# Moving work between engines in the start of a fused attention and expert kernel

## The chip, the cores and the metric

One NeuronCore of a Trainium2 chip runs the whole program; the other cores are idle. The metric is the device time of one execution in microseconds (us), as the median of several runs. Below, PE is TensorE (matmuls), ACT is ScalarE, DVE is VectorE, POOL is GpSimd, and SP is SyncE, which only issues DMAs.

## The reference

Three stages follow each other. The first is a linear attention with a delta rule: for every head a state matrix is read by the query and then corrected by the key, step by step over 768 positions. The second is a gated product of three matmuls, the third a mixture of 8 experts, where each token goes to one expert.

```python
for t in range(S):
    kt, vt, bt = (k_n[:, :, t], v[:, :, t], beta[:, :, t, None])
    y[:, :, t] = np.einsum('bhd,bhde->bhe', q[:, :, t], state)
    v_old = np.einsum('bhde,bhd->bhe', state, kt)
    state = state + bt[:, :, :, None] * np.einsum('bhd,bhe->bhde', kt, vt - v_old)
...
h = a * b @ w3              # a = x @ w1, b = x @ w2
return (h @ w_out)
...
e_idx = np.argmax(logits, axis=1)   # logits = x @ w_gate + modality_bias
out[mask] = gate_w[mask, None] * (np.maximum(x[mask] @ w1[e], 0.0) @ w2[e])
```

B = 4 batches, H = 8 heads, S = 768 positions, D = 48 per head; 3072 tokens of 384, inner width 1024.

## The kernel before, in words

**Attention in chunks.** The 768 positions are cut into 12 steps of 64, and two steps make a unit (6 units). Within a unit the recurrence becomes a triangular system for each of 64 pairs of heads and chunks. `gram` forms the products of keys on PE and copies them, negated, into `An`. `inverse` inverts the 32x32 diagonal blocks on DVE: it transposes the blocks (`Ab`), takes the norms of the keys from the diagonal (`ss`, a square root on ACT, then a chain of small operations for `r`), scales by beta (`bt`), and then runs 31 pairs of operations (`tmp`, then `T`), a product and a sum each, both with two SBUF inputs. At the end T is multiplied by beta and transposed back into `An` and, a second time, into `TT`. `merge1` and `merge2` make 64x64 blocks out of the 32x32 ones with matmuls (`pe`, `pf`) and copies of their results. `inverse` is a generator: each `yield` ends a step, and the callers say how many steps are taken where.

**One attention step s** is a chain: `chain_k` (keys times state, subtracted from the values that `scaled` multiplied by the key norms; result R), `chain_u` (TT times R into X), `chain_y` (the output, with the masked query products W, into yT and from there by DMAs into x), and `chain_s` (the new state). `masked` multiplies keys by queries on PE (`pq`) and writes the strictly causal part to W, by a DVE product with a 0/1 mask.

**The fused loop.** `moe1(i)` treats 256 tokens in 8 blocks f: 18 matmuls `pAB`, a product on DVE, and 6 matmuls `px` that run two blocks behind. Ahead of each block `slot(i + 1, f)` puts one piece of attention step i + 1. PLAN and PLAN1 say how many steps of the next unit's inverse go into each block (PLAN1 for the first token group). Then follow the experts (`moe2`), which the change does not touch.

**The startup** (line 522 on) must have the weights and attention step 0 ready before `moe1(0)`. It goes through a list of 36 loads: 8 pieces of w_out, 16 of w3, 12 of w1 and w2. Tick n takes one: `scalar(n + 1)` (two ACT passes that turn the 64-bit words of the next piece into fp32 parts), `vector(n)` (two DVE operations that merge them), `flush(n)` (copies that are now due) and `use(n)` (matmuls). `do[n]` adds the attention pieces to tick n: steps of the first inverse in ticks 1, 4, 6 and, by START0, 8 to 16; merge1, merge2 and the chain of step 0 from tick 17 on, one per tick (CHAIN); the second unit's key products at FC + 9 + GRAMS, that is in ticks 19 to 22; steps of the second inverse (WORK1) in the last four ticks; the routing constants in ticks 9 to 11. `split` puts a matmul piece into one tick and its copies into the next. REST says how many ticks are left to the first blocks of `moe1(0)`: two before.

**The order of the work** is set by hand: `Engine` (line 74) chains every instruction of an engine to the one before it, so each engine, SP and POOL too, runs its instructions in exactly the order in which the program issues them. POOL has little in its queue and so runs ahead of the others. PSUM tiles of one tag alternate between two buffers.

Of the kernel before, what the change touches and what calls it, by code (L numbers as in the profile page):

```python
# [15 lines left out]
AF = mybir.ActivationFunctionType  # L16
# [37 lines left out]
MID = (0,) * 5 + (0, 0, 1) + (2, 2, 2, 1, 1, 1, 1, 2)  # L54
PLAN1 = (3, 4, 4, 4, 5, 4, 4, 2)
WORK1 = (1, 1, 1, 1)
AHEAD, W0 = 8, 0
CHAIN, GRAMS = (1, 1, 1, 1, 1, 1), (2, 3, 4, 5)
START0 = (4, 4, 4, 4, 4, 4, 4, 4, 2)

REST = (1, 1)
EARLY = (4, 2)
# [41 lines left out]
class Kernel:  # L104
# [182 lines left out]
    def gram(self, u, a):  # L287

        nc, a1, ps = self.nc, self.a1, self.ps
        st = self.st[u]
        if "An" not in st:
            st["An"] = a1.tile([P, NU, C], F32, tag=f"An{(u + 1) % 2 if u else 0}", name="An")
        An, kT = st["An"], st["kT"]
        pg = ps.tile([P, HP, C], F32, tag="ps", name="pg")
        for n in range(HP):
            for h in range(2):
                o, w = (1 - h) * C, h * C  # L300
                nc.tensor.matmul(pg[o:o + C, n], kT[w:w + C, a + n], kT[w:w + C, a + n], start=True, stop=True)
        yield
        nc.scalar.activation(An[:, a:a + HP], pg, AF.Copy, scale=-1.0)

        for h in range(2):
            o = h * C + 32
            nc.scalar.activation(An[o:o + 32, a:a + HP, 0:32], pg[o:o + 32, :, 32:64], AF.Copy, scale=-1.0)
# [9 lines left out]
    def scaled(self, s):  # L317
        u, c = divmod(s, US)
        vt = self.st["v", s]
        self.nc.gpsimd.tensor_tensor(out=vt, in0=vt, in1=self.st[u]["r"][:, c * NP:(c + 1) * NP].unsqueeze(2).to_broadcast([P, NP, D]), op=ALU.mult)  # L320

    def inverse(self, u):
# [6 lines left out]
        nc.gpsimd.memset(T, 0.0)  # L329
        nc.gpsimd.memset(T.rearrange("p a b -> p (a b)")[:, 0:1024:33], 1.0)  # L330
        nc.vector.transpose(Ab.rearrange("n j i -> n i j"), An[:, :, 0:32].rearrange("j n i -> j i n"))

        ss, r, r2, rb = (a2.tile([P, 32], F32, tag=x, name=x) for x in ("ss", "r", "r2", "rb"))
        nc.vector.tensor_scalar(out=ss, in0=Ab.rearrange("p a b -> p (a b)")[:, 0:1024:33], scalar1=-1.0, scalar2=0.0, op0=ALU.mult, op1=ALU.max)
        nc.scalar.activation(r, ss, AF.Sqrt)
        yield
# [10 lines left out]
        st["r"] = rb  # L347
        nc.vector.tensor_tensor(out=Ab, in0=Ab, in1=bt.unsqueeze(2).to_broadcast([P, 32, 32]), op=ALU.mult)
        yield
        tmp = a1.tile([P, 256], F32, tag="tmp", name="tmp")  # L350
        for j in range(31):
# [5 lines left out]
            yield  # L357
        nc.vector.tensor_tensor(out=T, in0=T, in1=bt.unsqueeze(1).to_broadcast([P, 32, 32]), op=ALU.mult)

        nc.vector.transpose(An[:, :, 0:32].rearrange("i n c -> i c n"), T)  # L360
# [9 lines left out]
    def merge1(self, u):  # L370

        nc, A, todo = self.nc, self.st[u]["An"], []
        for c in range(0, NU, NP):
            pe = self.ps.tile([P, NP, 32], F32, tag="ps", name="pe")
            for n in range(NP):
                for h in range(2):
                    a, bb = h * C, h * C + 32
                    nc.tensor.matmul(pe[bb:bb + 32, n], A[a:a + 32, c + n, 32:64], A[a:a + 32, c + n, 0:32], start=True, stop=True)
            todo.append((c, pe))
        yield  # L380
        for c, pe in todo:
            for h in range(2):
                bb = h * C + 32
                nc.scalar.copy(A[bb:bb + 32, c:c + NP, 0:32], pe[bb:bb + 32])

    def merge2(self, u):
# [9 lines left out]
        for c, pf in todo:  # L396
            for h in range(2):
                a = h * C
                nc.scalar.copy(TT[a:a + 32, c:c + NP, 32:64], pf[a:a + 32])

# [8 lines left out]
    def masked(self, s):  # L409
# [13 lines left out]
        for a, pq in todo:  # L423
            for h in range(2):
                o = (1 - h) * C
                nc.vector.tensor_tensor(out=W[o:o + C, h, a:a + HP], in0=pq[o:o + C], in1=mb[o:o + C], op=ALU.mult)

# [23 lines left out]
    def chain_u(self, s):  # L451
# [10 lines left out]
        for a, pu in todo:  # L462
            for h in range(2):
                o = (1 - h) * C
                nc.scalar.copy(X[o:o + C, h, a * D:(a + HP) * D], pu[o:o + C])

    def chain_s(self, s):
# [10 lines left out]
        for a, pS in todo:  # L478
            for h in range(2):
                w = h * C  # L480
                if s == 0:
                    nc.scalar.copy(X2[w:w + D, h, a * D:(a + HP) * D], pS[w:w + D])
                    continue
# [3 lines left out]
    def chain_y(self, s):  # L487
# [15 lines left out]
        for a, py in todo:  # L503
            nc.scalar.copy(yT[:, a:a + HP], py)
            p0, p1 = a // B, (a + HP) // B
# [16 lines left out]
    def startup(self):  # L522
# [153 lines left out]
        for x in range(0, NU, HP):  # L676
            do.setdefault(FC + len(START0) + GRAMS[x // HP], []).append(lambda x=x: split(self.gram(1, x)))
        do.setdefault(t, []).append(lambda: setattr(self, "work", self.inverse(1)))
        for n, k in enumerate(WORK1, NSTART - len(WORK1)):
            do.setdefault(n, []).extend([lambda: next(self.work)] * k)  # L680
        rs = self.routing_setup()
        for x in range(3):
            do.setdefault(FC + 1 + x, []).append(lambda: next(rs, None))
        do.setdefault(t + 3, []).append(lambda: self.parts_x(0))
# [653 lines left out]
```

## Time and profile before

| | |
|---|---|
| Median of 3 runs | 857.78 us (857.75 to 859.2) |
| The profiled execution | 855.77 us, span 854.0 us |
| Busy over the span | PE 796.9, DVE 613.7, ACT 409.6, POOL 162.7 us |
| Mean granted clock of PE | 0.966 |

The span runs from the first to the last instruction of the profiled execution; its own time is 1.8 us longer. A wait is put down to what came last before the waiting instruction started. Times of matmuls are modelled, so a busy PE is not PE at its peak. The startup takes the first 129 us; the fused loop runs to about 610 us, the experts to the end.

### The profile page before, as it was taken

To read this page: it belongs to the slowest core of one execution; us is meant where nothing else is said; L and a number is where in the kernel's file an instruction comes from. 1 tells how busy PE (TensorE), PEld (TensorE's weight loads), DVE (VectorE), ACT (ScalarE), POOL (GpSimd) and SP (SyncE) were. 2 spreads that over 40 slices of the span, in tenths; PEclk is the share of its full clock that TensorE was granted. 3 is DMA by queue.
4 is the path that set the end of the run, shared out by engine and by line. 5 is a ranking of instruction groups with operands and counts; after the bars stand their busy time and mean duration, and the time that the engine had idled before them with its cause. 6 is when DMAs were issued, how large, how long until landed. Compare 5 with 4: busy or idle time off the path is not lost.

```text
span 854.0 us, 24817 instructions
## 1 busy us (share of the span) xinstructions
PE 796.9 (93%) x10223; PEld 739.6 (87%) x10223; DVE 613.7 (72%) x1512; ACT 409.6 (48%) x863; POOL 162.7 (19%) x174
## 2 busy tenths in 40 slices
PE   3977879989999999999999999999899999999994
PEld 3844638988999999999999999999899999999983
DVE  3897399969866986698669874457786678667651
ACT  6525964462445344624462444335555565655541
POOL 5000300010001000100010000003244564545420
PEclk8588979999999999999999999999999999999998
DMA  9835434303220322032202121028457768667620
GB/s 301 289 102 186 126 98 135 83 17 85 71 82 6 98 71 83 21 87 80 68 26 78 39 64 40 2 90 264 128 157 247 243 229 267 227 211 249 223 63 6
DMA packets 48777, 105.42 MB, mean 123 GB/s; under 512 B 9412, under 2 KB 28756, under 8 KB 48656
## 3 DMA queue, kind: packets, MB, share of 16 engines
q1 hardware_dynamic: 41424, 88.35, 33.5%
q0 software_dynamic: 4064, 11.06, 3.8%
q10 hardware_dynamic: 3168, 4.34, 1.4%
q8 instruction: 82, 1.34, 0.7%
q14 instruction: 39, 0.32, 0.1%
HBM read 89.15 MB, written 10.63 MB: 117 GB/s over the span
## 4 chain that ended last, share of the span: by engine, by line
PE 62%; DVE 8%; issue 8%; POOL 4%; ACT 1%; DMA 1%; SPq 0%; POOLq 0%; ACTq 0%; DVEq 0%
PE pAB L84 23%; PE px L84 14%; PE ph L84 7%; PE spy L84 4%; PE py L84 2%; PE pq L84 2%; PE pk L84 2%; PE pu L84 2%; PE pS L84 2%; POOL w1l L84 2%; PE pg L84 1%; PE pe L84 1%; DVE Tt L84 1%; POOL out_dram L84 1%; DVE tmp L84 1%
## 5 line engine op out<-in xcount | busy, mean ns | idle before, releaser
L84 PE MATMUL pAB<-x,w 128*128 128x256 f32 x1728 | 231.3, 288 | 0.0
L84 PEld LDWEIGHTS pAB<-x,w 128*128 128x128 f32 x1728 | 214.6, 192 | 4.1
L84 ACT CAST ch<-a 128x256 fp32r<-128x256 f32 x96 | 38.9, 406 | 117.7 <-DVE a L84 117.7
L84 ACT COPY a<-pAB 128x256 f32<-128x256 f32 x96 | 35.7, 372 | 124.5 <-PE pAB L84 118.4
L84 DVE TENSOR_TENSOR a<-a,pAB 128x256 f32<-128x256 f32 x96 | 39.9, 416 | 73.6 <-ACT a L84 73.4
L84 PE MATMUL ph<-sxh,w1h 128*128 128x256 f32 x288 | 82.1, 285 | 0.5 <-DVE hl L84 0.5
L84 PE MATMUL ph<-sxh,w1l 128*128 128x256 f32 x288 | 80.8, 281 | 0.0
L84 PE MATMUL ph<-sxl,w1h 128*128 128x256 f32 x288 | 80.8, 280 | 0.0
L84 ACT ACTIVATE hh<-ph 128x256 fp32r<-128x256 f32 x96 | 37.0, 385 | 89.1 <-PE ph L84 88.7
L84 DVE TENSOR_TENSOR Tt<-tmp,Tt 128x31 f32<-128x31 f32 (+15 forms) x186 | 63.8, 343 | 6.6 <-DVE tmp L84 0.2
L84 DVE SCALAR_TENSOR_TENSOR hl<-ph,hh 128x256 fp32r<-128x256 f32 x96 | 40.2, 419 | 39.0 <-ACT hh L84 37.7
L84 DVE TENSOR_TENSOR w2l<-r,w2h 128x768 fp32r<-128x768 f32 x56 | 59.3, 1071 | 12.3 <-ACT w2h L84 12.1
L84 DVE TENSOR_TENSOR tmp<-Ab,Tt 128x31 f32<-128x31 f32 (+15 forms) x186 | 65.4, 352 | 3.2
L84 PE MATMUL px<-w34h,ch 128*128 128x392 f32 x192 | 65.8, 343 | 0.8 <-DVE w34l L84 0.8
L84 PE MATMUL px<-w34h,cl 128*128 128x392 f32 x192 | 65.3, 340 | 0.0
L84 PE MATMUL px<-w34l,ch 128*128 128x392 f32 x192 | 65.2, 339 | 0.0
L84 POOL TENSOR_TENSOR w1l<-r,w1h 128x512 fp32r<-128x512 f32 x39 | 50.5, 1313 | 50.4 <-ACT w1h L84 50.2
L84 POOL TENSOR_TENSOR vt<-vt,rb 128x768 f32<-128x768 f32 x12 | 18.2, 1519 | 201.6 <-DMA vt<-in_v_dram 117.7
L84 PEld LDWEIGHTS ph<-sxh,w1h 128*128 128x128 f32 x288 | 54.3, 188 | 1.3 <-DVE hl L84 1.1
L84 PE MATMUL pw<-wosW,TT 128*128 128x392 f32 x80 | 37.0, 605 | 19.5 <-DVE TT L84 19.2
L84 DVE TENSOR_TENSOR cl<-a,ch 128x256 fp32r<-128x256 f32 x96 | 40.4, 421 | 19.6 <-ACT ch L84 18.8
L84 PEld LDWEIGHTS ph<-sxh,w1l 128*128 128x128 f32 x288 | 54.3, 189 | 0.0
(262 smaller groups left out, 1742.9 us busy)
## 6 DMA issues: line engine op xcount, KB each, us to landing
r<-in_e_w_dram SPq DMA_DIRECT2D x42, 512.0 KB, 4.7
r<-in_e_w_dram SPq DMA_DIRECT2D x56, 384.0 KB, 3.9
raw<-in_w_dram SPq DMA_DIRECT2D x25, 512.0 KB, 4.8
kT<-in_kt_dram SPq DMA_DIRECT2D x12, 512.0 KB, 4.1
W<-in_q_dram SPq DMA_DIRECT2D x24, 256.0 KB, 4.4
vt<-in_v_dram SPq DMA_DIRECT2D x12, 384.0 KB, 4.6
kb<-in_kb_dram SPq DMA_DIRECT2D x12, 384.0 KB, 3.5
x2d<-xr ACTq DMA_DIRECT2D x22, 192.5 KB, 3.0
```

The lines of the kernel that those rows point to most:

```text
L84: x = f(*a, **kw)
```

## The change

T starts with beta on its diagonal instead of 1, and Ab is scaled by beta along its other axis, so the product of T and beta at the end goes. For units 0 and 1 one more `yield` stands ahead of the square root. In the first three masks ACT copies the products and POOL zeroes the non-causal part in place. In step 0 (and unit 0's merges) one of two copies goes to DVE; so do the full-size copies of the second unit's key products and the scaling of the first values. Key products move to ticks 19 and 20, routing constants to ticks 17 to 19, the second inverse starts in tick 24 with one step per tick, and three ticks instead of two are left to `moe1(0)`.

```diff
-PLAN1 = (3, 4, 4, 4, 5, 4, 4, 2)
-WORK1 = (1, 1, 1, 1)
+PLAN1 = (3, 3, 3, 4, 4, 4, 3, 2)
+WORK1 = (1,)*9
-CHAIN, GRAMS = (1, 1, 1, 1, 1, 1), (2, 3, 4, 5)
+CHAIN, GRAMS = (1, 1, 1, 1, 1, 1), (2, 2, 3, 3)
-REST = (1, 1)
+REST = (1, 1, 1)
...
-        nc.scalar.activation(An[:, a:a + HP], pg, AF.Copy, scale=-1.0)
+        if u == 1:
+            nc.vector.tensor_scalar(out=An[:, a:a + HP], in0=pg, scalar1=-1.0, scalar2=None, op0=ALU.mult)
+        else:
+            nc.scalar.activation(An[:, a:a + HP], pg, AF.Copy, scale=-1.0)
...
-        self.nc.gpsimd.tensor_tensor(out=vt, in0=vt, in1=self.st[u]["r"][:, c * NP:(c + 1) * NP].unsqueeze(2).to_broadcast([P, NP, D]), op=ALU.mult)
+        (self.nc.gpsimd if s else self.nc.vector).tensor_tensor(out=vt, in0=vt, in1=self.st[u]["r"][:, c * NP:(c + 1) * NP].unsqueeze(2).to_broadcast([P, NP, D]), op=ALU.mult)
...
-        nc.gpsimd.memset(T.rearrange("p a b -> p (a b)")[:, 0:1024:33], 1.0)
...
+        if u < 2:
+            yield
         nc.scalar.activation(r, ss, AF.Sqrt)
...
-        nc.vector.tensor_tensor(out=Ab, in0=Ab, in1=bt.unsqueeze(2).to_broadcast([P, 32, 32]), op=ALU.mult)
+        nc.vector.tensor_tensor(out=Ab, in0=Ab, in1=bt.unsqueeze(1).to_broadcast([P, 32, 32]), op=ALU.mult)
+        nc.vector.tensor_copy(T.rearrange("p a b -> p (a b)")[:, 0:1024:33], bt)
...
-        nc.vector.tensor_tensor(out=T, in0=T, in1=bt.unsqueeze(1).to_broadcast([P, 32, 32]), op=ALU.mult)
...
-                nc.scalar.copy(A[bb:bb + 32, c:c + NP, 0:32], pe[bb:bb + 32])
+                (nc.vector.tensor_copy if u == 0 and h else nc.scalar.copy)(A[bb:bb + 32, c:c + NP, 0:32], pe[bb:bb + 32])
...
-                nc.scalar.copy(TT[a:a + 32, c:c + NP, 32:64], pf[a:a + 32])
+                (nc.vector.tensor_copy if u == 0 and h else nc.scalar.copy)(TT[a:a + 32, c:c + NP, 32:64], pf[a:a + 32])
...
+                if s < 3:
+                    nc.scalar.copy(W[o:o + C, h, a:a + HP], pq[o:o + C])
+                    nc.gpsimd.affine_select(out=W[o:o + C, h, a:a + HP], in_=W[o:o + C, h, a:a + HP], pattern=[[0, HP], [1, C]], compare_op=ALU.is_gt, fill=0.0, base=0, channel_multiplier=-1)
+                    continue
                 nc.vector.tensor_tensor(out=W[o:o + C, h, a:a + HP], in0=pq[o:o + C], in1=mb[o:o + C], op=ALU.mult)
...
-                nc.scalar.copy(X[o:o + C, h, a * D:(a + HP) * D], pu[o:o + C])
+                (nc.vector.tensor_copy if s == 0 and h else nc.scalar.copy)(X[o:o + C, h, a * D:(a + HP) * D], pu[o:o + C])
...
-                    nc.scalar.copy(X2[w:w + D, h, a * D:(a + HP) * D], pS[w:w + D])
+                    (nc.vector.tensor_copy if h else nc.scalar.copy)(X2[w:w + D, h, a * D:(a + HP) * D], pS[w:w + D])
...
-            nc.scalar.copy(yT[:, a:a + HP], py)
+            (nc.vector.tensor_copy if s == 0 and a else nc.scalar.copy)(yT[:, a:a + HP], py)
...
-        do.setdefault(t, []).append(lambda: setattr(self, "work", self.inverse(1)))
+        do.setdefault(FC + len(START0) + GRAMS[-1] + 2, []).append(lambda: setattr(self, "work", self.inverse(1)))
...
-            do.setdefault(FC + 1 + x, []).append(lambda: next(rs, None))
+            do.setdefault(FC + 9 + x, []).append(lambda: next(rs, None))
```

## Rows read from the trace of the kernel before

**Rows 1.** Busy time by stretch: start:end, length, PE, PEld, DVE, ACT, POOL, clock, DMA.
```profile
30.00:76.00 46.00, 36.01 (x161) 22.49 (x160) 43.66 (x96) 15.48 (x30) 1.84 (x1) 0.80 0.53 174
76.00:132.00 56.00, 46.25 (x726) 31.86 (x727) 36.97 (x65) 43.73 (x82) 6.56 (x11) 0.88 0.45 131
132.00:175.00 43.00, 39.65 (x632) 36.96 (x630) 40.20 (x96) 17.40 (x41) 3.51 (x3) 1.00 0.29 82
222.00:537.00 315.00, 315.00 (x5425) 298.41 (x5420) 235.08 (x665) 136.27 (x289) 13.47 (x13) 1.00 0.20 59
```

**Rows 2.** Waits of PE after 126 us: total, times, longest.
```profile
PE pe L84 <- DVE An L84: 2.6, 1, 2.6
```

**Rows 3.** Timeline of DVE, 21 to 36 us: start, us.
```profile
21.57 0.17 DVE L84 TENSOR_SCALAR r<-r 128x32 f32<-128x32 f32 x1
...
23.68 1.22 DVE L84 TENSOR_TENSOR Ab<-Ab,bt 128x1024 f32<-128x1024 f32 x1
...
29.98 0.69 DVE L84 SCALAR_TENSOR_TENSOR TT<-spare,TT 128x512 int32<-128x512 int32 x1 [0.89 <-ACT TT L84]
...
33.55 2.56 DVE L84 SCALAR_TENSOR_TENSOR TT<-spare,TT 128x512 int32<-128x512 int32 x2
```

**Rows 4.** Timeline of DVE, 49 to 75 us.
```profile
49.12 0.17 DVE L84 COPY rsc<-pmod 128x24 f32<-128x24 f32 x1
...
50.49 0.16 DVE L84 TENSOR_SCALAR cnt<-ei 128x8 f32<-128x8 f32 x1
...
52.00 2.79 DVE L84 TENSOR_TENSOR W<-pq,mask 64x512 f32<-64x512 f32 x4
...
69.59 1.23 DVE L84 TENSOR_TENSOR Tt<-Tt,bt 128x1024 f32<-128x1024 f32 x1
70.85 1.90 DVE L84 STREAM_TRANSPOSE An<-Tt 128x1024 f32<-128x1024 f32 x1
72.61 1.86 DVE L84 STREAM_TRANSPOSE TT<-Tt 128x1024 f32<-128x1024 f32 x1
```

**Rows 5.** Timeline of ACT, 15 to 25 us.
```profile
15.41 1.28 ACT L84 ACT_TABLE_LOAD   x1
...
24.72 0.48 ACT L84 COPY TT<-wot 128x384 f32<-128x384 f32 x1 [3.01 <-PE wot L84]
```

**Rows 6.** Groups of POOL's instructions, affine selects: busy us, mean ns.
```profile
L84 POOL TENSOR_SCALAR_AFFINE_SELECT tri<-tri 128x128 bf16<-128x128 bf16 x1 | 0.6, 574 | 0.1
...
L84 POOL TENSOR_SCALAR_AFFINE_SELECT mask<-mask 64x64 f32<-64x64 f32 x2 | 0.5, 233 | 0.1
...
masks.py:199 POOL TENSOR_SCALAR_AFFINE_SELECT ident<-ident 128x128 f32<-128x128 f32 x1 | 0.3, 282 | 0.0
```

**Rows 7.** POOL's product and memset, and DVE beside them; a group of DVE's.
```profile
135.38 1.61 POOL L84 TENSOR_TENSOR vt<-vt,rb 128x768 f32<-128x768 f32 x1 [29.34 <-DMA vt<-in_v_dram]
149.02 1.94 POOL L84 MEMSET TT<- 32x1024 f32 x2 [12.03 <-DVE w L84]
...
135.58 1.55 DVE L84 TENSOR_TENSOR tmp<-Ab,Tt 128x112 f32<-128x112 f32 x1
...
149.22 0.40 DVE L84 TENSOR_TENSOR Tt<-tmp,Tt 128x231 f32<-128x231 f32 x1
...
L84 DVE TENSOR_TENSOR tmp<-Ab,Tt 128x112 f32<-128x112 f32 x2 | 0.5, 274 | 0.1
```

**Rows 8.** Groups of ACT's copies, 76 to 132 us: busy us, mean ns.
```profile
L84 ACT COPY An<-pe 32x512 f32<-32x512 f32 x4 | 2.3, 578 | 1.6 <-PE pe L84 1.5
...
L84 ACT COPY X<-pu 64x384 f32<-64x384 f32 x4 | 1.9, 474 | 0.1
```

**Rows 9.** Timeline of DVE: the first R of the fused step.
```profile
132.09 1.01 DVE L84 TENSOR_TENSOR R<-vt,pk 128x384 f32<-128x384 f32 x2
```

**Rows 10.** Busy time and clock behind the stall, columns as in rows 1.
```profile
178.00:180.00 2.00, 2.00 (x11) 2.00 (x10) 1.12 (x1) 1.96 (x3) 0.76 (x1) 0.50 0.00 0
180.00:182.00 2.00, 2.00 (x12) 2.00 (x11) 0.22 (x1) 1.61 (x3) 1.76 (x3) 0.68 0.00 0
```

## The prediction, made before the changed kernel ran

> **What bounds the kernel now.** I read the busy time of each engine in five stretches first [rows 1]. From 222 to 537 us TensorE is busy for all 315 us, so whatever VectorE (DVE) saves there has no place to show. The change can only pay before that: from 30 to 76 us DVE is busy 43.66 of 46 us; from 76 to 132 us ScalarE (ACT) is busy 43.73 of 56 us and DVE 36.97; from 132 to 175 us DVE has 40.20 of 43 us. In this last stretch the list of waits names one stall that ends the stage: TensorE waits 2.6 us for An, the transposed inverse of the second unit [rows 2]. So there are three stages, and the sum is made stage by stage: A, the first unit's inverse on DVE; B, the ticks with both engines; C, the first fused step, which ends at that stall.
>
> **Stage A, to the first unit's second transpose (ends 74.47 us) [rows 3, 4].** An instruction's cost is the distance to the next start.
> - The four mask products leave DVE: they start at 52.00 and the next work at 54.72, so -2.7 us.
> - The routing constants leave for later ticks: 49.12 to 50.56, -1.4 us, and a cast of 0.1.
> - The product of T and beta goes: 69.59 to 70.85, -1.3 us. The copy of beta to T's diagonal (128x32) is priced by the nearest 128x24 copy, 0.17 (it stands in the 3.4 below). POOL's memset of that diagonal goes too; POOL idles there.
> - The scaling of the first values leaves GpSimd (POOL). While it ran, two of DVE's merges took 2.56 us where the pair at 29.98 takes 1.33 (the next work starts at 31.31): -1.2 us here, +0.95 in stage B, where DVE does it.
> - The chain behind the square root, 21.57 to 24.81, now comes two ticks later. Before, it lay in a stretch in which DVE waited for ACT anyway: cost nothing. That cover is gone. The square root now stands behind the copy that waits for TensorE until 24.72 and pays its table load of 1.28 us there [rows 5]; with the next tick's two ACT passes the merge of that tick starts at 27.5 us. Then 1.15 (merge) + 3.4 (chain and diagonal) + 1.15 (merge) = 33.2 us for the start of the tick that started at 29.98: +3.2 us. The first step of the inverse (0.4) moves behind it: +0.4.
> - For the mask, ACT copies four times 64x512 (0.55 each, in a stretch where it is idle two thirds of the time [rows 1]) and POOL runs four affine selects, which no row shows at this size. 64x64 took 0.23 and 128x128 0.28 us [rows 6]: 0.77 ns per further element, so 0.6 us for 512. From above: the product of 768 elements on POOL took 1.61 us, 1.07 for 512 [rows 7]; and the bf16 select of 128 elements took 0.57 us [rows 6], by its rate 2.3 us. From below: 0.3, the row for 128 elements. I take 0.6, since the two fp32 selects are the same operation and type.
> - A select may hold up DVE. When POOL ran its product at 135.38 us, a DVE product of two SBUF inputs took 1.55 us where the same one elsewhere takes 0.27: it lost 1.28 of POOL's 1.61 us. During a POOL memset at 149.02 the neighbours kept 0.40 us [rows 7]. A select reads SBUF like the product, and DVE has only such two-input work in that tick, so I charge 0.87 x 0.6 x 4 = +2.1 us.
>
> The Trainium skill, page "SBUF — State Buffer", section "Who interferes with whom", says that a DVE instruction with two SBUF inputs contends with a GpSimd instruction that reads SBUF, though not with one that only writes it, and that the loser waits for the whole instruction. Both rows agree with it. By that rule the sum keeps the 2.1; by the memset's row alone it would drop them.
>
> An: -2.7 - 1.5 - 1.3 - 1.2 + 3.2 + 0.4 + 2.1 = -1.0 us. The second transpose has moved behind one more tick's merge (1.3 us), so it ends at 74.47 - 1.0 + 1.3 = 74.8 us, +0.3. So the 6.7 us taken off DVE are nearly eaten up.
>
> **Stage B, to the first R of the fused step (132.09 us) [rows 8, 9].** Off ACT: two copies each from pe and pf (0.58), from pu and pS (0.47), and one of y and four of the key products, priced like pe's: 9 x 0.58 + 4 x 0.47 = 7.1 us. Onto DVE the same thirteen, priced by its 64x512 product from PSUM (2.79 for four [rows 4]), less where there are 384 elements, 0.57 on the mean: about 7.4; the values 0.95; the routing 1.5; four more steps of the second inverse (2.5) and its diagonal (0.2). Off DVE: one tick that moves behind the start (1.9) and the merge that now lies before the transpose (1.3). Together +9.4, on 36.97 busy and 19.0 idle. Both queues are in order, so these don't simply fill the idle time: the copies on DVE stand ahead of the next tick's merge and wait for TensorE, and the values and routing stand between merge2's copies and the merge whose result TensorE needs next. Going through the 17 ticks with these durations I find DVE idle for 8 to 9 us (2.6 of them behind ACT's copies of TT), the first step's products about 2 us later than now, and the last ticks DVE-bound as before. R starts at 131.4 us: -0.7 us against now. POOL's DMAs of the first x start with the y copies, about 3 us later, and are needed 9 us after they land: nothing. The routing step's counters and memsets on POOL, at 10 to 12 us now, queue there behind the first mask and the memset of TT, and POOL idles from 57 us on: nothing. Key products earlier cost nothing: their keys are loaded in tick 13, and ACT's small copies of them, which must now wait for DVE's full-size ones, are in the 8 to 9 us. The weight tick that moves behind the start takes its load and buffer with it, used a block before the product that needs it: nothing.
>
> **Stage C, to the stall.** DVE: the masks go (2.8), T times beta (1.3), four steps already done (2.5); one tick more comes (1.9). New: in the third block ACT makes four mask copies (2.2 us) ahead of the copy that DVE's next product waits for, so DVE idles 1.8 us; three of the four selects fall into that, and one costs 0.5. POOL's product of 1.61 us stalls DVE as before. -2.8 - 1.3 - 2.5 + 1.9 + 1.8 + 0.5 = -2.4, and -0.7 from B: An is ready 3.1 us earlier. ACT's six copies of key products ahead of the last block's copy take about 0.5 of it back. TensorE's other work before pe ends at 172.7 us now (175.28 less its 2.6 idle); its fifth block waits for the second mask, which I find ready 1 us sooner, so 171.7. An still decides: pe starts at about 172.7 instead of 175.28: **-2.6 us**. Behind the stall the granted clock fell to 0.50 (1.2 GHz) in 178 to 180 us and to 0.68 in the next two [rows 10], which costs 2 x 0.50 + 2 x 0.32 = 1.6 us of full-clock time. With an idle time of 1.0 instead of 2.6 us I count a quarter of that as saved, -0.4. The third mask moves to ACT and POOL in the same way, one step later; TensorE gets its first half sooner and its second, behind four selects, later: 0. From there TensorE is full, so **the sum is -3.0 us**. The five later inverses save 1 us of DVE each: nothing, as said.
>
> The profiled execution took 855.77 us (span 854.0), 2.0 below the median of the three runs, 857.78. So I expect 852.8 for a like execution and a median of **854.8 us**. About 0.2%, 1.7 us, is what can be told from no change.
>
> **The rivals.**
> 1. DVE is not held by the selects (they behave like the memset). For: the only selects in the trace ran while DVE was idle, so no row shows them together. Against: the product's rows. Then 2.1 us come back in A, and the stall in C nearly vanishes with its slow clock (-1.2, what is left of the 1.6): 851.5 us.
> 2. DVE's order is the new bound in B: it stands at the head of each copy until TensorE is done, and the ticks lose what the lighter ACT gained. For: 19.0 us of idle time go to a queue with 9.4 us more work, and the products of the first step come later already in my sum. Against: ACT's 43.73 busy of 56 us [rows 1]. If the idle left is 11 instead of 8.5 us: 857.3, no change.
> 3. Slower: POOL's selects are slow. Place: the first mask in stage A, and the second, whose result TensorE needs in block five. Each 0.25 us more per select costs 4 x 0.25 x 0.87 = 0.87 us at the first mask; from 1.5 us per select the gain is gone. By the bf16 row's rate (2.3 us) the first mask costs 4 x 1.7 x 0.87 = 5.9 us more: 860.7 us. For: that row, and that the new select runs over a pattern of two levels, which none of the rows has. Against: the two fp32 rows.
> 4. The change doesn't do what it says: the square root's load stays early, or the cover of the r chain is not gone. Then 3.2 us come back: 851.6 us.
>
> **How the numbers follow.** Forecast 0.45, first rival 0.15, second 0.20, third 0.15, fourth 0.05. The forecast's own range is 853 to 857: the select between 0.3 and 0.9 us, and 1 us of idle time either way. Faster by more than 0.2% (under 856.1): the forecast but for its upper edge (0.07), the first and the fourth: 0.38 + 0.15 + 0.05 = 0.58. Within 0.2% (to 859.5): that edge and the second but for 0.02, 0.25. Slower: the third and that 0.02, 0.17. The range takes in the first and second rival and the third up to 1.6 us per select: 850.5 to 859.5.
>
> **What would show it.** In the changed profile: DVE's chain behind the square root at about 28.6 us and a second table load near 25; four selects near 52 to 56 us of 0.6 us, with DVE steps of about 1 us beside them; both transposes done near 74.8; from 76 to 132 us ACT below 40 and DVE above 44 busy us of 56; the first block's R near 131; pe at 172 to 173. Selects over 1.5 us, or an R later than 134, would make the prediction wrong; an unchanged pe wait of 2.6 us would say that C's bound is another.

## The result, and the profile after

The changed kernel takes 863.65 us (median of 5, 861.93 to 864.0) against 857.78 us (now 5 runs, with the same median): ratio 1.0059, 95% interval 1.0043 to 1.0075. It is slower by 0.6%, and lies above the range. The profiled execution took 863.65 us, its span is 861.8 us, 7.8 longer than before. Busy time by stretch of the changed kernel (columns as in [rows 1]):

```profile
30.00:76.00 46.00, 38.78 (x167) 24.16 (x166) 43.18 (x96) 18.20 (x35) 6.59 (x16) 0.80 0.52 174
76.00:132.00 56.00, 41.06 (x641) 26.67 (x639) 45.53 (x85) 33.43 (x64) 6.40 (x10) 0.84 0.37 109
132.00:175.00 43.00, 39.29 (x616) 36.88 (x615) 36.32 (x85) 20.92 (x45) 5.95 (x7) 0.92 0.39 109
```

The busy sums came as forecast: from 76 to 132 us ACT is below 40 and DVE above 44. PE has 5.2 us less work in that stretch, and in the next one the granted clock is 0.92 instead of 1.00. Where the time is lost shows in PE's first blocks, the timeline of PE in the changed kernel (start, length, what ended the idle time before):

```profile
133.83 4.58 PE L84 MATMUL pAB<-x,w 128*128 128x256 f32 x36
...
150.69 1.22 PE L84 MATMUL pAB<-x,w 128*128 128x256 f32 x8
153.73 1.10 PE L84 MATMUL pAB<-x,w 128*128 128x256 f32 x7 [1.82 <-DVE w L84]
156.72 1.36 PE L84 MATMUL pAB<-x,w 128*128 128x256 f32 x3 [1.89 <-ACT w L84]
...
159.97 3.22 PE L84 MATMUL pg<-kT 64*64 64x64 f32 x64
163.12 2.42 PE L84 MATMUL pAB<-x,w 128*128 128x256 f32 x18
...
182.35 2.21 PE L84 MATMUL pe<-An 32*32 32x32 f32 x128
```

and the same engine in the kernel before:

```profile
129.27 4.58 PE L84 MATMUL pAB<-x,w 128*128 128x256 f32 x36
...
147.99 2.42 PE L84 MATMUL pAB<-x,w 128*128 128x256 f32 x18
...
175.28 2.21 PE L84 MATMUL pe<-An 32*32 32x32 f32 x128 [2.55 <-DVE An L84]
```

The first blocks start 4.56 us later (133.83 against 129.27). From there to pe it takes 48.52 us instead of 46.01, 2.51 more. From pe to the end it takes 679.45 instead of 678.72, 0.73 more. The sum is the 7.8 us by which the span grew.

The stall that the prediction built on [rows 2] is gone: pe waits for nothing. A new one stands in the fifth block, which waits for its weights `w` twice, 3.7 us in all. Behind that wait the granted clock is 0.54 from 157 to 163 us:

```profile
157.00:163.00 6.00, 6.00 (x73) 5.28 (x73) 5.69 (x15) 2.39 (x6) 1.89 (x2) 0.54 0.27 69
```

so that pg takes 3.22 us, where 64 matmuls of the same form took 2.16 at 87.41 us in the same execution. Behind the old stall, too, the clock was slow for a few microseconds [rows 10].

### The profile page after: what moved, and what is told of

Same layout as the page of the kernel before. It is cut to its first block, busy times and chain, and to the rows that moved or that the text cites. A ratio compares the mean times of both kernels' runs of the same rounds, so it can differ in the third digit from the quotient of the medians.

```text
span 861.8 us, 24822 instructions
## 1 busy us (share of the span) xinstructions
PE 801.1 (93%) x10223; PEld 742.0 (86%) x10223; DVE 610.2 (71%) x1514; ACT 409.2 (47%) x862; POOL 168.7 (20%) x179
## 4 chain that ended last, share of the span: by engine, by line
PE 70%; DVE 12%; issue 6%; DMA 5%; ACT 4%; POOL 1%; SPq 0%; ACTq 0%; POOLq 0%; DVEq 0%
PE pAB L84 22%; PE px L84 14%; PE ph L84 9%; PE spy L84 5%; DVE TT L84 3%; PE pk L84 3%; PE py L84 3%; PE pu L84 2%; PE pg L84 2%; PE pq L84 2%; PE pw L84 2%; PE pS L84 2%; DVE tmp L84 2%; DMA wg<-in_w_gate_dram 2%; DVE Tt L84 1%
## 5 line engine op out<-in xcount | busy, mean ns | idle before, releaser
L84 DVE TENSOR_TENSOR tmp<-Ab,Tt 128x31 f32<-128x31 f32 (+15 forms) x186 | 67.6, 364 | 2.8
L84 PE MATMUL pw<-wosW,TT 128*128 128x392 f32 x80 | 40.0, 654 | 21.3 <-DVE TT L84 21.0
L84 PEld LDWEIGHTS ph<-sxl,w1h 128*128 128x128 f32 x288 | 54.6, 190 | 0.0
```

The source lines that it names most:

```text
L84: x = f(*a, **kw)
```

## The experiments

One row is one kernel. The ratio is to the kernel before on the same chip (its medians there were 858.46, 858.75, 858.25 and 858.99 us for the four groups). R, first blocks and pe are the starts of the first R, of the double pAB and of the first pe behind it, in the profiled execution. Medians of different groups are compared by their ratios.

| kernel | median | ratio, 95% interval | R | first blocks | pe | blocks to pe |
|---|---|---|---|---|---|---|
| before | 857.78 | | 132.09 | 129.27 | 175.28 | 46.01 |
| changed | 863.65 | 1.0059 (1.0043 to 1.0075) | 134.94 | 133.83 | 182.35 | 48.52 |
| two ticks left | 858.12 | 1.0009 (0.9989 to 1.003) | 138.20 | 137.87 | 179.38 | 41.51 |
| square root early | 859.51 | 1.0019 (0.9995 to 1.0043) | 131.19 | 129.86 | 177.25 | 47.39 |
| split by tile | 861.94 | 1.0049 (1.0026 to 1.0073) | 133.41 | 132.06 | 180.72 | 48.66 |
| second values on DVE | 859.27 | 1.001 (0.9992 to 1.0029) | 136.21 | 134.14 | 182.75 | 48.61 |
| two masks back | 864.23 | 1.0065 (1.004 to 1.0091) | 133.69 | 132.34 | 181.34 | 49.00 |
| two ticks, early root | 854.68 | 0.9943 (0.9921 to 0.9965) | 133.52 | 132.18 | 173.69 | 41.51 |
| four costs taken back | 852.82 | 0.993 (0.9911 to 0.9949) | 132.50 | 130.10 | 171.61 | 41.51 |
| before + beta first | 854.47 | 0.9949 (0.993 to 0.9968) | 130.31 | 127.41 | 172.25 | 44.84 |
| before + third tick | 859.04 | 1.0006 (0.9995 to 1.0016) | 130.6 | 127.52 | 178.11 | 50.59 |
| four back, no sharing | 851.39 | 0.9901 (0.9883 to 0.9918) | 130.11 | 127.80 | 169.31 | 41.51 |
| four back, masks on DVE | 854.42 | 0.9937 (0.9921 to 0.9954) | 136.4 | 134.98 | 177.42 | 42.44 |
| four back, two masks on DVE | 855.78 | 0.9957 (0.9941 to 0.9973) | 133.8 | 132.32 | 174.68 | 42.36 |
| changed, no sharing | 859.39 | 1.0008 (0.9992 to 1.0024) | 131.34 | 129.99 | 178.48 | 48.49 |
| the same, second values on DVE | 860.16 | 1.0021 (1.0006 to 1.0036) | 131.6 | 129.19 | 178.35 | 49.16 |

The last column is the clearest reading. In the four kernels in which TensorE waits for nothing in this stage it is 41.51 us to the hundredth: TensorE's own time for the stage. Against it the kernel before loses 4.5 us and the changed kernel 7.0. The times of R and of the first blocks are less certain: each is read from one execution, and that of the kernel before was 2 to 3 us faster than its medians.

### Two ticks left to the first blocks instead of three

```diff
-REST = (1, 1, 1)
+REST = (1, 1)
```

> The changed kernel with two ticks left to the first fused step instead of three (REST = (1, 1)), as before. Theory W: the loss is TensorE's wait for the second-half weights in the fifth block (1.8 + 1.9 us) and the slow clock behind it, because the third tick puts the last weights two DVE blocks too late. Then both waits on w go, the first R moves from 134.9 to about 137 us (one tick more before it, 1.9 us), and the time falls by about 3 us to 860.5. Rival S: the late start is the loss and the wait only follows from it. Then the waits stay above 2 us in sum and the time rises by up to 2 us to 865.5.

The stage takes 41.51 instead of 48.52 us, and every block of it runs in one piece (timeline of PE):

```profile
154.72 2.41 PE L84 MATMUL pAB<-x,w 128*128 128x256 f32 x18
160.14 2.42 PE L84 MATMUL pAB<-x,w 128*128 128x256 f32 x18
...
179.38 2.21 PE L84 MATMUL pe<-An 32*32 32x32 f32 x128
```

From the fifth pAB to the sixth it is 5.42 us here and 12.43 in the changed kernel (150.69 to 163.12): there lie all 7.0 us of the difference, 3.7 of them waits and the rest the slow clock behind. The first blocks start 4.0 us later. One more tick lies before them, which the third-tick run below puts at 1.75 us; and in this execution the clock was low earlier, too (eight pw matmuls took 4.29 us instead of 2.90, last section). What is left, 3.0 us, is what pe gains; the ratio falls by 0.5%. So the weights are on the path. (REST also shifts a little how the pieces of w1 and w2 are mixed with those of w3 in the list of loads; that comes with the tick here and below.)

### The square root without the extra step

```diff
-        if u < 2:
+        if u == 1:
             yield
         nc.scalar.activation(r, ss, AF.Sqrt)
```

> The changed kernel without the extra step ahead of the square root in unit 0 (only unit 1 keeps it). Theory: the chain behind the square root lies on DVE's path in its new place. The first transposes end 3 to 4.5 us sooner (An at 68, TT at 70 instead of 74.4 us), the first R comes about 3 us sooner (132), the w waits shrink by as much, and the time falls by 3 us to 860.5. Rival: stage B waits for ACT and TensorE, and swallows the gain: R moves by under 1 us and the time by under 1 us.

An's transpose starts at 65.50 us instead of 69.36, 3.9 us sooner; R and the first blocks come 3.75 and 3.97 sooner. The waits for `w` stay (1.81 and 1.91 us), where I had them shrink by as much. The 3.9 us are the pair furthest apart, though: with the same work up to there, An's transpose starts at 68.34 to 69.36 us in the seven versions with the step and at 65.50 to 66.89 in the five without it, and the middle ones are 2.7 us apart. So the extra step costs about 2.7 us, up to 3.9, and in this pair the whole of it reaches the end of stage B.

### Shared copies split by whole PSUM tile

One of the four places, the others in the same way (the fifth, y, already went by whole tiles):

```diff
-                (nc.vector.tensor_copy if u == 0 and h else nc.scalar.copy)(TT[a:a + 32, c:c + NP, 32:64], pf[a:a + 32])
+                (nc.vector.tensor_copy if u == 0 and c else nc.scalar.copy)(TT[a:a + 32, c:c + NP, 32:64], pf[a:a + 32])
```

> The changed kernel with the shared copies divided by PSUM tile (ACT takes the first tile, DVE the second) instead of by half of one tile. Theory: two engines that read one PSUM tile are kept one after the other (in the profile DVE's copy starts 0.03 to 0.04 us after ACT's ends, five times). Divided by tile they overlap: each of the three pairs of merge2, chain_u and chain_s ends about 0.5 us sooner, R comes 1 to 1.5 us sooner, and the time falls by 1 to 1.5 us to 862.4. Rival: DVE would have come to these copies no sooner anyway (in-order queue, TensorE's end): R and the time move by under 0.5 us.

In the changed kernel the two engines take half a tile each, and DVE waits for ACT (timelines of ACT, then of DVE):

```profile
86.06 0.57 ACT L84 COPY TT<-pf 32x512 f32<-32x512 f32 x1 [3.87 <-PE pf L84]
87.07 0.57 ACT L84 COPY TT<-pf 32x512 f32<-32x512 f32 x1 [0.44 <-PE pf L84]
...
86.66 0.69 DVE L84 COPY TT<-pf 32x512 f32<-32x512 f32 x1 [3.04 <-ACT TT L84]
87.68 0.69 DVE L84 COPY TT<-pf 32x512 f32<-32x512 f32 x1 [0.33 <-ACT TT L84]
```

DVE's copy starts 0.03 to 0.04 us after ACT's has ended, here and with X: the two halves run one after the other. With a tile each, DVE waits for PE instead, and the copies overlap a little:

```profile
84.96 1.16 ACT L84 COPY TT<-pf 32x512 f32<-32x512 f32 x2 [3.72 <-PE pf L84]
...
85.98 1.38 DVE L84 COPY TT<-pf 32x512 f32<-32x512 f32 x2 [3.32 <-PE pf L84]
```

R comes 1.5 us sooner, of which 1.0 lies ahead of the transpose to TT (71.42 against 72.46 us), before any shared copy. So the split is worth about 0.5 us at R, and since the intervals of the two ratios overlap, the time doesn't show it. DVE still stands 3.32 us at the head of its queue.

### The scaling of the second values on VectorE

```diff
-        (self.nc.gpsimd if s else self.nc.vector).tensor_tensor(...)
+        (self.nc.gpsimd if s > 1 else self.nc.vector).tensor_tensor(...)
```

> The changed kernel with the scaling of the second values on DVE as well, instead of POOL. Theory: POOL's product at 108.4 us held a DVE merge for 2.73 instead of 0.69 us. On DVE it costs 0.95 us, in the fused step's first block, so R comes 2.0 us sooner and pays 0.95 back just before it: R about 1 us sooner, the time 1 us less, 862.6. Rival: DVE was waiting for ACT there anyway: the time is unchanged or 1 us more (864.6).

The reason to try it is a merge in the changed kernel, beside POOL's product (timelines of POOL and DVE):

```profile
108.44 1.49 POOL L84 TENSOR_TENSOR vt<-vt,rb 128x768 f32<-128x768 f32 x1
...
107.03 0.69 DVE L84 SCALAR_TENSOR_TENSOR TT<-spare,TT 128x512 int32<-128x512 int32 x1
107.76 2.73 DVE L84 SCALAR_TENSOR_TENSOR TT<-raw,TT 128x512 int32<-128x512 int32 x1
```

The second half of the merge took 2.73 instead of 0.69 us; with the product on DVE it takes 0.69. The ratio falls by 0.5%, some 4 us, where I had 1 us. But the profiled execution was the slowest of the twelve (864.07 us) and starts its first blocks at 134.14 us, no sooner, so it doesn't show where the others gained, and that stays open. The last pair of experiments tries the same edit again.

### The masks of steps 1 and 2 back on VectorE

```diff
-                if s < 3:
+                if s < 1:
```

> The changed kernel, with the masks of steps 1 and 2 back on VectorE (a product with the 0/1 mask, 2.8 us for four); only the first mask stays on ScalarE and GpSimd. Theory (the late weights cost stage C, the masks only little): VectorE loses its idle time of 2.1 us behind ScalarE's mask copies and the stall beside the select, and gets 2.8 us of products back, so the last weight pieces land within 1 us of where they do in the changed kernel (the last at 156.8 us), pAB waits for them as long (1.8 + 1.9 us), and the short waits of py and pr for W (0.7 and 0.5) go: 862 to 864 us, ratio to the kernel before 1.004 to 1.007. Rival (the masks on ScalarE and GpSimd are what made stage C late): the waits for the weights go below 1 us and the time falls by 3 us or more, to 860.5 or less.

The theory held in the main: the waits for `w` are 1.1 and 1.9 us (I had 1.8 and 1.9), DVE finishes the last piece at 156.1 us, and the ratio of 1.0065 is not told apart from the changed kernel's. The waits for W didn't go: pr now waits 2.1 us for DVE's. Putting the second and third mask back doesn't mend stage C.

### Two of the costs taken back together, and four

The edits above together: first two ticks and the early root, then also the split by tile and the second values on DVE.

> The changed kernel with two edits taken back together: two ticks instead of three are left to the first blocks, and the square root of the first unit comes without the extra step ahead of it. Alone they gave 858.1 and 859.5 us. Theory (two separate costs: the late weights lie in stage C, the later square root in stages A and B): they add, the first R comes at 133.5 to 135.5 us (one more tick before it than in the changed kernel, and the inverse 3.9 us sooner), pe starts 41 us behind it, 174.5 to 176.5 us, no wait of pAB for w: 853 to 856 us. Rival (both repair the same delay): no more than the better of the two, 857 to 859 us.

> The changed kernel with all four costs taken back: two ticks left to the first blocks, the square root without the extra step, the shared copies split by whole PSUM tile instead of by half of a tile, and the scaling of the second values on VectorE. Theory (the costs add): R 1 us sooner than with the first two alone, 132.5 to 134.5 us, and 852 to 855 us, the fastest of all. Rival (the last two are lost in waits that end later): the same as with two edits, within 1 us; or VectorE, with two products of values more (0.95 us each against 1.5 on GpSimd), is what R waits for, and it is slower than with two edits by 1 us.

Both came as the theory said (pe a little sooner, at 173.69 us). The two costs add: taken back alone they are worth 0.5% and 0.4%, together 1.2%. Two more edits bring R another 1.0 us forward and the median from 854.68 to 852.82, though here the two intervals overlap. Both versions beat the kernel before.

### The beta-first inverse alone, on the kernel before

```diff
-        nc.gpsimd.memset(T.rearrange("p a b -> p (a b)")[:, 0:1024:33], 1.0)
-        nc.vector.tensor_tensor(out=Ab, in0=Ab, in1=bt.unsqueeze(2).to_broadcast([P, 32, 32]), op=ALU.mult)
+        nc.vector.tensor_tensor(out=Ab, in0=Ab, in1=bt.unsqueeze(1).to_broadcast([P, 32, 32]), op=ALU.mult)
+        nc.vector.tensor_copy(T.rearrange("p a b -> p (a b)")[:, 0:1024:33], bt)
-        nc.vector.tensor_tensor(out=T, in0=T, in1=bt.unsqueeze(1).to_broadcast([P, 32, 32]), op=ALU.mult)
```

> The kernel before, with only the beta-first inverse (T starts with beta on its diagonal, Ab scaled along its other axis, no product of T and beta at the end). Theory: the 1.3 us of the product go and 0.1 to 0.2 us for the copy to the diagonal come, so the second transpose ends at 73.1 to 73.5 us instead of 74.5, the first R comes up to 1.1 us sooner, the second unit's An 1.1 us sooner again, and the wait of pe for An shrinks from 2.6 to 0.5 to 1.5 us: 855.5 to 857.5 us against 857.8. Rival (the ticks of stage B are bound elsewhere, so nothing of it reaches the first R, and the second unit's 1.1 us alone count): 857 to 858 us, not told from no change.

It gains 4.3 us (858.75 to 854.47), where I had 0.3 to 2.3. This is the timeline of DVE, then of PE:

```profile
68.69 1.93 DVE L84 STREAM_TRANSPOSE An<-Tt 128x1024 f32<-128x1024 f32 x1
...
172.25 2.21 PE L84 MATMUL pe<-An 32*32 32x32 f32 x128 [1.32 <-DVE An L84]
```

An is transposed 2.16 us sooner than in [rows 4]: 1.26 for the product, and 0.9 from the merge at 29.08 us, which started at 29.98 [rows 3] where DVE waited for ACT; that part needn't be the edit's. Most of it reaches the first blocks (1.86 us), and the wait of pe falls from 2.55 to 1.32 us (the stage from 46.01 to 44.84). So 3.0 us of the gain stand in the profile up to pe: the product that goes from the first inverse and the one from the second count one after the other. Behind the shorter wait the clock stays up, too: the 18 pAB matmuls take 2.41 us, where they took 3.86 in the kernel before (the line is in the part on the prediction).

### The third tick alone, on the kernel before

```diff
-REST = (1, 1)
+REST = (1, 1, 1)
```

> The kernel before, with only the third tick left to the first blocks. Theory (the tick that moves behind the start makes the second half of the weights late by itself): the first R comes 1.5 to 2.5 us sooner than 132.1, the last piece of the weights, which lands at 148.9 us in the kernel before, lands at 149.5 to 152 us, and the fifth block's pAB waits 2 to 5 us for it where it waited for nothing. VectorE has the same work up to An, so pe starts within 1.5 us of 175.3 and the time is 857.5 to 860 us: no gain from an earlier start. Rival (the weights are late only because of the masks and the later inverse of the changed kernel): pAB waits under 1 us, pe starts with the same wait for An or less, and the time is 855.5 to 857.5 us.

This is the cleanest test of the step that failed, with no mask or copy moved. First the kernel before, DVE's last piece of the weights:

```profile
148.18 0.69 DVE L84 TENSOR_TENSOR w<-TT,w 128x512 fp32r<-128x512 f32 x1
```

then DVE with the third tick, and PE's fifth block there:

```profile
147.86 0.68 DVE L84 TENSOR_TENSOR w<-TT,w 128x512 fp32r<-128x512 f32 x1
152.44 0.68 DVE L84 TENSOR_TENSOR w<-TT,w 128x512 fp32r<-128x512 f32 x1
...
146.36 1.22 PE L84 MATMUL pAB<-x,w 128*128 128x256 f32 x8
148.60 1.09 PE L84 MATMUL pAB<-x,w 128*128 128x256 f32 x7 [1.02 <-DVE w L84]
152.41 1.35 PE L84 MATMUL pAB<-x,w 128*128 128x256 f32 x3 [2.72 <-ACT w L84]
```

In the kernel before the last piece is finished at 148.87 us, within the fifth block, which starts at 147.99 and reads it in the last 3 of its 18 matmuls: by an estimate (15/18 of 2.42 us into the block, 150.0) about 1 us of slack. With one more tick it is finished at 153.1, and the block waits 3.7 us. The first blocks start 1.75 us sooner, the stage takes 50.59 us, pe comes 2.8 us later (I had expected at most 1.5), and the median is that of the kernel before within 0.16%: an earlier start paid for with a later wait.

### The version with four costs back: sharing, masks

First all shared copies back on ACT (one of the five places is shown), then the three masks on DVE, then two of them (`s < 1`).

```diff
-                (nc.vector.tensor_copy if u == 0 and c else nc.scalar.copy)(TT[a:a + 32, c:c + NP, 32:64], pf[a:a + 32])
+                nc.scalar.copy(TT[a:a + 32, c:c + NP, 32:64], pf[a:a + 32])
```

```diff
-                if s < 3:
+                if s < 0:
```

> The version with all four costs taken back, with the shared copies of the first step and of the first unit's merges all on ScalarE again. Theory (two engines that take a PSUM tile each do gain): pe's, pf's, pu's, pS's and y's second copies come 0.5 to 1.2 us later each on the chain, R at 133 to 135 us, 853.5 to 855.5 us against 852.8. Rival (the ticks are bound elsewhere, so where the copies lie is worth nothing): R within 0.5 us of 132.5 and the time within 0.6 us of 852.8.

> The version with all four costs taken back, with the first three masks back on VectorE (one product of 0.7 us for each of the four tiles). Theory (the masks on ScalarE and GpSimd gain what they take off VectorE, less the 1.3 us that the selects hold its steps): the second transpose of the first unit ends 1.2 to 1.8 us later than 69.2, R 1 to 1.8 us later than 132.5, pr of step 1 waits 2 us for W; 854 to 856 us. Rival (the selects hold VectorE as long as the products took, or the 1.3 us are lost again by the first R): R within 0.5 us of 132.5 and 852.3 to 853.3 us.

> The version with all four costs taken back, with only the masks of steps 1 and 2 back on VectorE. Theory (in stage C of that version pe no longer waits for An, so VectorE's 2.8 us are covered by TensorE's work, and only W comes later): R within 0.5 us of 132.5, An up to 2.5 us later, py and pr wait up to 2.5 us for W in place of 0.7; 852.5 to 854 us. Rival (TensorE waits again for An because VectorE is the bound of the stage): a wait of pe of 1 us or more, and 854.5 us or more.

The first fell on neither side: without sharing the median is 851.39 us, the lowest of all, and R comes at 130.11 instead of 132.50. The intervals overlap (0.9901 and 0.993), so this pair alone doesn't prove a gain; the next section shows it in the changed kernel. Where I had looked for a gain of parallel copies there is none.

With the masks on DVE the median is 1.6 us higher, as the theory had it, but the ratios, 0.9937 and 0.993, are not told apart. The transpose to TT starts at 70.14 instead of 67.34 us, 2.8 later, where I had 1.2 to 1.8; against the latest of the five versions with the early root it is 1.5 (68.69). R at 136.4 is not used: this profile is of its slowest execution (858.22 us). With two masks on DVE the time is 855.78, where I had said 852.5 to 854, and pe waits for nothing, so the rival's reason isn't there either. Of the 3 us against 852.82 the profile shows 0.85 in the stage itself (42.36 instead of 41.51; a wait of 0.36 us for `w34l` is in it), and 2.2 ahead of the first blocks, where the edit changes nothing; pr's wait of 2.1 us for W lies behind pe. What the masks are worth stays open.

### The changed kernel without the sharing

The same edit in the changed kernel (there `u == 0 and h` goes), first alone, then with the second values on DVE as well.

> The changed kernel, with the shared copies of the first step and of the first unit's merges all on ScalarE again and nothing else taken back. Theory (a copy at the head of VectorE's queue stands until TensorE is done, and the shared copies cost the ticks more than ScalarE's lighter load gives): with the four other costs taken back this moved the first R from 132.5 to 130.1 us; here the first block starts 1.5 to 3 us sooner than at 133.8 us, the waits for the weights stay 3.5 to 4 us, and the time is 860 to 862.3 us. Rival (the gain seen there was of that execution, or needs the second values on VectorE too): first block at 133.3 to 134.3 us, 863 to 864.5 us.

> The changed kernel, with the shared copies all on ScalarE again and the scaling of the second values on VectorE. Theory (the product on GpSimd holds VectorE for about 2 us on the way to the first R, and VectorE needs 0.95 for it, so 1 us is to be had beside the copies): the first block starts 0.5 to 1.5 us sooner than with the copies alone, 858.7 to 861.3 us. Rival (that stall is covered by a wait which ends later): the first block and the time within 0.5 us of the version with the copies alone.

Without the sharing the first blocks start at 129.99 instead of 133.83 us, more than I expected, and the ratio falls from 1.0059 to 1.0008 (863.65 and 859.39 us), with intervals clear of each other. This is DVE's timeline around pf without sharing:

```profile
80.09 1.41 DVE L84 SCALAR_TENSOR_TENSOR TT<-spare,TT 128x512 int32<-128x512 int32 x2
81.42 0.95 DVE L84 TENSOR_TENSOR vt<-vt,rb 128x768 f32<-128x768 f32 x1
86.57 0.18 DVE L84 COPY rsc<-pmod 128x24 f32<-128x24 f32 x1 [4.20 <-PE pmod L84]
...
88.01 0.68 DVE L84 SCALAR_TENSOR_TENSOR TT<-spare,TT 128x512 int32<-128x512 int32 x1
```

and in the changed kernel:

```profile
82.20 1.42 DVE L84 SCALAR_TENSOR_TENSOR TT<-spare,TT 128x512 int32<-128x512 int32 x2
...
88.40 0.96 DVE L84 TENSOR_TENSOR vt<-vt,rb 128x768 f32<-128x768 f32 x1
89.39 0.18 DVE L84 COPY rsc<-pmod 128x24 f32<-128x24 f32 x1
...
90.83 0.68 DVE L84 SCALAR_TENSOR_TENSOR TT<-spare,TT 128x512 int32<-128x512 int32 x1
```

DVE waits either way. But with the copies it stands before pf, and the values, the routing and the merge come after; without them the values run during the wait. The next merge comes 2.8 us sooner, 0.6 of it from the transpose (71.83 against 72.46). TensorE needs what that merge makes for its eight pw matmuls, and waits for it 0.53 us instead of 2.73 (lines in the last section).

With the second values on DVE too, the first blocks come 0.8 us sooner, but the wait for `w` is longer, so pe starts at the same time (178.35 and 178.48) and the medians are not told apart. The rival held as to the time. There was less to take back here, too: with the copies on ACT alone, POOL's product runs from 105.59 us, DVE waits for ACT during more than half of it, and the one DVE step beside it takes 1.22 us instead of 0.68, a loss of 0.5 us and not of 2.04.

## Why the prediction was wrong

**Stage A was right, to 0.4 us in this execution.** The transpose to TT ended at 74.44 us, where I had 74.8; in the six other versions with the same work up to there it ended at 73.4 to 73.9. The timelines of ACT, DVE and POOL in the changed kernel:

```profile
25.36 1.28 ACT L84 ACT_TABLE_LOAD   x1
...
28.86 0.17 DVE L84 TENSOR_SCALAR r<-r 128x32 f32<-128x32 f32 x1
...
52.78 3.19 POOL L84 TENSOR_SCALAR_AFFINE_SELECT W<-W 64x512 f32<-64x512 f32 x4 [42.78 <-ACT W L84]
...
53.15 0.75 DVE L84 TENSOR_TENSOR tmp<-Ab,Tt 128x252 f32<-128x252 f32 x1
53.93 0.75 DVE L84 TENSOR_TENSOR Tt<-tmp,Tt 128x252 f32<-128x252 f32 x1
...
56.27 0.41 DVE L84 TENSOR_TENSOR tmp<-Ab,Tt 128x240 f32<-128x240 f32 x1
...
69.36 1.94 DVE L84 STREAM_TRANSPOSE An<-Tt 128x1024 f32<-128x1024 f32 x1
72.46 1.98 DVE L84 STREAM_TRANSPOSE TT<-Tt 128x1024 f32<-128x1024 f32 x1
```

The table load and the chain behind the square root stand where I put them (28.86 for 28.6). I charged the lost cover with 3.2 + 0.4 us; it measures 2.7 to 3.9. The selects took 0.80 us each instead of 0.6. Four DVE steps beside them took 0.75 instead of 0.42, so they lost 1.3 us and not 2.1: a longer select, but 0.33 us lost to each instead of 0.52. With errors of both signs among its terms, that the sum came out this close is in part luck. (My factor of 0.87 was too high already by its own row: 1.28 of 1.61 us is 0.80.)

**Stage B failed by 3.5 us**: R came at 134.94, not 131.4, later than the 134 that I had named as a sign of being wrong. The step is "Going through the 17 ticks with these durations I find DVE idle for 8 to 9 us". From the end of the transpose to R DVE was idle for 10.9 us and busy for 49.6, where my sum has 8.5 and 48.0 (38.6 in the kernel before, and 9.4 more). The 1.6 us of busy time are one merge that POOL's product for the second values held for 2.04 us: I moved the ticks without looking at what that product then falls beside. The idle time is the mechanism that the sentence ahead of the step names (copies that stand ahead of the next merge and wait for TensorE), but I gave it no price at each copy, and no term for two halves of a tile that are copied one behind the other. Taking those copies back gives R at 131.34, 3.6 us sooner, of which 0.6 lies ahead of them. This is the second rival, at 0.20, and its 11 us of idle time is what came. But idle time is not the measure that I took it for: without the copies DVE is idle for 15.0 us from the transpose to R, and R is sooner. What counts is what stands behind the wait in the queue.

**Stage C failed by the step "used a block before the product that needs it: nothing"** (it stands at the end of B in the prediction). I looked at where the last piece of weights is used, not at when DVE finishes it: in the kernel before that was 148.87 us, for a block that began at 147.99. No row of mine held this. In place of nothing, the late weights cost 7.0 us between the fifth block and the sixth, 3.7 of them waits, against 4.0 us by which the changed kernel's first blocks start sooner than with two ticks.

The gain that I forecast in this stage was there, and larger: 4.5 us (46.01 against 41.51), where I had 1.9 from R to pe. The kernel before shows of what it is made (timeline of PE):

```profile
141.21 0.45 PE L84 MATMUL px<-w34h,ch 128*128 128x392 f32 x1 [0.78 <-DVE w34l L84]
146.91 1.15 PE L84 MATMUL py<-W,X 128*64 128x64 f32 x30 [0.29 <-DVE W L84]
...
177.42 3.86 PE L84 MATMUL pAB<-x,w 128*128 128x256 f32 x18
```

Against the version without sharing, block by block, 2.6 us are the stall of pe, 1.1 lie around the wait of px for `w34l`, which my sum doesn't have, and 0.8 around the wait of py for the second mask, where I had 1. An was to decide still, with 1.0 us of idle time left; in the four versions at 41.51 it doesn't. The slow clock is not in the 4.5 us: it lies behind pe, where the 18 matmuls at 177.42 took 3.86 us and take 2.42 without the stall. That is 1.4 us, of which I had counted 0.4.

**Behind pe** the span is 0.73 us longer instead of 0.4 shorter. The versions run from 678.0 to 681.2 us from pe to the end, so a term of this size is below what one profile tells.

**The rivals.** The selects did hold DVE, they weren't slow (0.80 us, far from the 1.5 at which the third rival decides), and the change did what it says. The one on the slow side named GpSimd; it should have been the weights, whose lateness I could have read from two rows.

So three edits, and the second values that stayed on POOL while the ticks around them moved, cost more than the rest gave. Taken back one at a time in the changed kernel, the third tick, the root's extra step, the sharing and the second values on POOL are worth 0.5%, 0.4%, 0.5% and 0.5%. They don't simply add: all four together give 1.6% (1.0059 to 0.9901), and the last is worth nothing once the sharing is gone, so its 0.5% is not explained. The beta-first inverse alone gives 0.5%. What remains of the change without the four runs at 0.9901 of the kernel before; what the masks, the earlier key products, the later routing constants and the earlier second inverse have in that isn't shown.

## What to carry to other kernels

Before work is moved past a start, read for each piece when it is finished and when its first reader begins; about 1 us of slack doesn't bear a tick. A share of an idle engine's time isn't free when its queue is in order: a copy that waits for TensorE holds everything issued behind it. Read a cost from more than one execution: one pair said 3.9 us where twelve say 2.7. And a stage's time without waits, the same to the hundredth in several versions, tells at once how much of a stage can be won.

## What the runs showed of the hardware

- A select of 64x512 and a DVE step of 252 columns shared the time: the steps began every 0.78 us, where one after the other they would take 0.70 + 0.42 = 1.12 (the four selects at 146.43 us took 2.81, most of it with DVE idle). The Trainium skill, page "SBUF — State Buffer", section "Who interferes with whom", says the loser waits for the whole instruction: the trace shows a loss on DVE, as it says, but of 0.33 us of a 0.80 us select.
- The granted clock in stage B differs between executions with the same PE work up to there. The same eight pw matmuls took 2.90 us in the changed kernel and 5.59 with the second values on DVE; the granted clock from 90 to 95 us was 1.00 and 0.62. Timelines of PE, first of the changed kernel:

```profile
92.30 2.90 PE L84 MATMUL pw<-wosW,TT 128*128 128x392 f32 x8 [2.73 <-DVE TT L84]
```

then with the second values on DVE:

```profile
92.10 5.59 PE L84 MATMUL pw<-wosW,TT 128*128 128x392 f32 x8 [2.72 <-DVE TT L84]
```

and in the changed kernel without the sharing:

```profile
89.47 2.90 PE L84 MATMUL pw<-wosW,TT 128*128 128x392 f32 x8 [0.53 <-DVE TT L84]
```

A difference of 2.7 us comes without any edit to these matmuls or to the wait ahead of them, and is as large as most costs sought here; the times of R and of the first blocks carry it. It goes with the sharing: in all ten versions with shared copies TensorE waits 2.6 to 2.7 us ahead of these eight matmuls, and in seven of them they then took 4.27 to 5.59 us; in the six without shared copies it waits 0.53 us at most, and they took 2.90 us in each. So part of what the sharing costs can be the clock; in the pair read here, the changed kernel and the same without sharing, it isn't, since both took 2.90.
